# Making every second group of down-projection weight rests on GpSimd in a chain of attention and two gated layers

## The chip, the cores and the metric

One core of a Trainium2 chip runs the whole kernel as one program. The metric is the device time of one execution in microseconds; before the change it is 900.63 us, the median of 3 runs (899.34 to 901.4).

## What is computed

Linear attention with random features, then two feed-forward layers on its output; all data are float32.

```python
# q, k, v: (4, 8, 576, 64); omega: (128, 64)
q_p, k_p = phi(q * scale), phi(k * scale)     # phi: exp of a projection on omega
kv, z = einsum("bhsm,bhsd->bhmd", k_p, v), k_p.sum(2)
x = einsum("bhsm,bhmd->bhsd", q_p, kv) / (einsum("bhsm,bhm->bhs", q_p, z) + 1e-6)
x = x.transpose(0, 2, 1, 3).reshape(2304, 512)
h = x @ w_in                                  # 512 -> 2048
x = (silu(h) @ w_out)                         # 2048 -> 512
g, val = x @ w_gate, x @ w_val                # 512 -> 1536 each
out = (silu(g) * val) @ w_out2                # 1536 -> 512
```

The weights come as 64-bit floats, of which the kernel makes float32.

## The kernel before

The attention takes the first 125 us or so. After it come four stages: an up stage (`up_phase`, x @ w_in), a down stage (`down_phase`, @ w_out), then the same for the second layer with w_gate and w_val, and w_out2. Each matrix product is done by Strassen's scheme in Winograd's form: seven products of half the size in each direction, run in `ORDER` 1, 5, 6, 2, 7, 3, 4. Each operand of a product is split in two parts for TensorE: a lead, which is the operand rounded to a shorter format (`hi`, a copy with ScalarE), and a rest, operand minus lead (`lo`, a subtraction, which writes over the operand). Three matmuls (lead by lead, lead by rest, rest by lead) then stand for one.

A down stage has two kinds of operands.

- The weights of product p, blocks of 128x256. `split_load` (L1244) makes them: SyncE loads a group of up to three blocks (128x768) from `wd_out` in device memory (L1248), ScalarE makes the lead (L1252) and VectorE the rest (L1256). In the first down stage a product has three groups (768, 768 and 512 wide, 21 in all), in the second two of 768 (14 in all). They are made once, stay for all tokens of the stage, and are put into slots of `ra`, `rb` and `rc` as the up stage frees them. Their making begins while the up stage before is at its end. `split_load` also makes the weights of the gate and value products (`w_load`, pieces of 128x448).
- The tokens' operands. `down_phase.split` (L1300 to L1324) treats them in pieces of 128x768 (two feature blocks by 384 tokens); a product has four pieces in the first stage, three in the second, numbered from 0 here. ScalarE makes the lead (L1300) and VectorE the rest (L1304). Where the next product's operand is a difference, VectorE also makes that, piece by piece, after the rest (L1324). SyncE loads the four operands B11, B12, B21, B22 (L1274); the differences T1 to T4 write over them.

A piece is used by 12 matmuls of 128x384 (L1441, six for each of two PSUM banks). Group g of the weights is wanted from the piece on that reaches its three blocks: in the first stage group 0 at piece 0, group 1 at piece 1 and group 2 at piece 3.

On the up stage's side L1091 and L1115 are ScalarE's copies and SiLUs, L1132 and L1148 VectorE's products and sums (most with one input in PSUM), L1100 the stores of its output. GpSimd has the sums of the weight conversion (L376), four a job.

The order on every engine is settled when the program is written. Work waits in streams (`wd` holds the weight loads and splits, `split` the operands, `conv` the conversions); `flush` takes from them, before each group of matmuls, what a model of the engines' clocks says can start soon. The model's costs for an element are in `fixed` (VectorE 0.00106 us, GpSimd 0.0021 us). Each engine then runs its own list in order, and waits for semaphores.

```python
        def lo(o, w):
            h, l = (cut(t, o, w) for t in take())
            nc.vector.tensor_sub(l, l.bitcast(F32), h.bitcast(F32))
```

Of the kernel before, what the change touches and what calls it, by code (L numbers as in the profile page):

```python
# [9 lines left out]
F32 = mybir.dt.float32  # L10
# [32 lines left out]
def kernel(  # L43
# [13 lines left out]
    nc = tc.nc  # L57
# [43 lines left out]
    def cut(t, o, n):  # L101
        return t[:, o : o + n]
# [8 lines left out]
    class Free:  # L111
# [11 lines left out]
        def take(self):  # L123
            assert self.q, f"no {self.name}"
            x, t = self.q.popleft()
            clk["slot"] = max(clk["slot"], t)
            return x
# [12 lines left out]
    def cost(kind, n):  # L140
        a, b = fixed[kind]
        return a + b * n
# [40 lines left out]
    def dma_cost(nbytes):  # L183
        return nbytes / 350e3
# [1036 lines left out]
    def down_ops(m):  # L1221

        fp = FP[m]
        nt = (fp + 2) // 3
        Wd = {}

        def load(p, g):
            o = OPA[PROD[p][0]]
            n = min(3, fp - 3 * g) * 256
            key = lambda *k: ("Wd", m, p, g, *k)  # L1230

            def take():
                if (p, g) not in Wd:
                    Wd[p, g] = (f_op.take(), f_op.take())
                return Wd[p, g]

            return split_load(
                take, n, wd_d[DNK[m]][o, :, g * 768 : g * 768 + n], key, (f_op, 2),
                [(DNK[m], 3 * g + i, "d", (0, 1, 1, 3, 3, 3, 3)[o]) for i in range(n // 256)],
            )  # L1240

        return Wd, [o for p in ORDER for g in range(nt) for o in load(p, g)]

    def split_load(take, n, src, key, slots, ins=(), parts=1):  # L1244


        def load():
            nc.sync.dma_start(out=cut(take()[1], 0, n).bitcast(F32), in_=src)  # L1248

        def hi(o, w):  # L1250
            h, l = (cut(t, o, w) for t in take())
            nc.scalar.activation(h, l.bitcast(F32), AF.Copy)  # L1252

        def lo(o, w):
            h, l = (cut(t, o, w) for t in take())
            nc.vector.tensor_sub(l, l.bitcast(F32), h.bitcast(F32))  # L1256

        ops = [Op("SP", dma_cost(P * n * 4), load, ins=ins, outs=[key("r")], slots=slots)]
        w = n // parts
        for o in range(0, n, w):  # L1260
            end = [key()] if o + w == n else []
            ops += [
                Op("ACT", cost("ACT", w), lambda o=o: hi(o, w), ins=[key("r")], outs=[key("hi", o)]),
                Op("DVE", cost("DVE", w), lambda o=o: lo(o, w), ins=[key("hi", o)], outs=[key("lo", o), *end]),
            ]
        return ops

# [287 lines left out]
    def w_load(k, ins=()):  # L1555
        def take():
            if (k, 0) not in W:
                W[k, 0] = (f_w.take(), f_w.take())
            return W[k, 0]

        return split_load(take, 1792, wu_d[k], lambda *x: ("W", k, 0, *x), (f_w, 2), ins, 4)
# [88 lines left out]
```

## Time and profile before

| | |
|---|---|
| median of 3 runs | 900.63 us (899.34 to 901.4) |
| profiled execution | 901.76 us, its span 900.0 us |
| TensorE busy | 876.9 us, 97% |
| VectorE busy | 628.9 us, 70% |
| ScalarE busy | 548.4 us, 61% |
| GpSimd busy | 161.4 us, 18% |
| TensorE's share of the chain that ended last | 85% |
| VectorE's share of it | 5% |
| first down stage | begins at about 306 us |
| second down stage | begins at about 760 us |

Times in the rows below are microseconds from the start of the span. A row of a timeline gives start, length, engine, line, operation, output and input; neighbours of one kind are merged, and a bracket at the end gives the idle time ahead of the row on its engine and what ended it. An instruction's listed length can begin while the one before it on its engine still runs.

### The profile page before, as it was taken

To read this page: it belongs to the slowest core of one execution; us is meant where nothing else is said; L and a number is where in the kernel's file an instruction comes from. 1 tells how busy PE (TensorE), PEld (TensorE's weight loads), DVE (VectorE), ACT (ScalarE), POOL (GpSimd) and SP (SyncE) were. 2 spreads that over 40 slices of the span, in tenths; PEclk is the share of its full clock that TensorE was granted. 3 is DMA by queue.
4 is the path that set the end of the run, shared out by engine and by line. 5 is a ranking of instruction groups with operands and counts; after the bars stand their busy time and mean duration, and the time that the engine had idled before them with its cause. 6 is when DMAs were issued, how large, how long until landed. Compare 5 with 4: busy or idle time off the path is not lost.

```text
span 900.0 us, 18108 instructions
## 1 busy us (share of the span) xinstructions
PE 876.9 (97%) x6887; PEld 853.0 (95%) x6887; DVE 628.9 (70%) x1016; ACT 548.4 (61%) x1166; POOL 161.4 (18%) x204
## 2 busy tenths in 40 slices
PE   8999999999999989999998999999999999999998
PEld 6787899999999989999998999999999998999998
DVE  3788778576654696785898898555565547968684
ACT  5898878776766764444466856454545356545553
POOL 0474922033441000000000034121212100000000
PEclk9999999999999999999999999999999999999999
DMA  6777448579999937427315557352534278281702
GB/s 200 244 259 240 159 162 271 186 243 303 295 329 343 399 136 220 131 72 237 114 59 181 191 176 243 113 193 99 189 109 154 89 241 285 94 242 44 241 1 71
DMA packets 105863, 170.08 MB, mean 189 GB/s; under 512 B 8752, under 2 KB 87984, under 8 KB 105776
## 3 DMA queue, kind: packets, MB, share of 16 engines
q1 hardware_dynamic: 104608, 168.33, 56.7%
q8 instruction: 54, 0.88, 0.4%
q10 hardware_dynamic: 1168, 0.59, 0.2%
q14 instruction: 33, 0.27, 0.1%
HBM read 107.02 MB, written 61.87 MB: 188 GB/s over the span
## 4 chain that ended last, share of the span: by engine, by line
PE 85%; DVE 5%; ACT 4%; DMA 3%; issue 2%; SPq 0%; DVEq 0%; ACTq 0%
PE ps L1074 45%; PE ps L1441 31%; PE ps L750 3%; PE ps L794 2%; PE ps L810 2%; ACT kq L766 2%; PE ps L841 1%; DMA rawq<-in_q 1%; DVE ra L1304 1%; DMA fa<-in_moe_w_in 1%; DMA fa<-in_moe_w_out 1%; DVE rc L1256 1%; DVE ra L423 1%; DMA ra<-wu_val 1%; DMA om<-in_omega 0%
## 5 line engine op out<-in xcount | busy, mean ns | idle before, releaser
L376 POOL TENSOR_TENSOR fa<-fa 128x256 f32<-128x256 f32 x136 | 111.4, 832 | 554.4 <-DVE fa L357 322.1
L1074 PE MATMUL ps<-ra 128*128 128x384 f32 x840 | 156.2, 335 | 3.5 <-ACT ps L1091 3.5
L1074 PE MATMUL ps<-rb,ra 128*128 128x384 f32 x840 | 157.2, 340 | 0.0
L1074 PE MATMUL ps<-rc,ra 128*128 128x384 f32 x840 | 157.0, 340 | 0.0
L1074 PEld LDWEIGHTS ps<-ra 128*128 128x128 f32 x840 | 146.7, 188 | 4.8 <-ACT ps L1091 4.8
L1074 PEld LDWEIGHTS ps<-rb,ra 128*128 128x128 f32 x840 | 148.8, 188 | 0.3 <-ACT ps L1091 0.3
L1074 PEld LDWEIGHTS ps<-rc,ra 128*128 128x128 f32 x840 | 148.7, 188 | 0.3 <-ACT ps L1091 0.2
L1091 ACT ACTIVATE ps<-ps 128x384 f32<-128x384 f32 x180 | 85.5, 476 | 86.3 <-PE ps L1074 80.1
L1300 ACT ACTIVATE ra<-fa 128x768 fp32r<-128x768 f32 x105 | 87.8, 844 | 81.0 <-PE ps L1441 64.6
L1148 DVE TENSOR_TENSOR fa<-fa,ps 128x384 f32<-128x384 f32 x120 | 66.3, 552 | 100.7 <-ACT ps L1091 73.1
L1304 DVE TENSOR_TENSOR ra<-fa,ra 128x768 fp32r<-128x768 f32 x105 | 100.5, 957 | 48.9 <-PE ps L1441 31.7
L1441 PE MATMUL ps<-ra,rb 128*128 128x384 f32 x720 | 128.5, 339 | 0.0
L1441 PEld LDWEIGHTS ps<-ra,rb 128*128 128x128 f32 x720 | 127.1, 188 | 0.5 <-DVE ra L1304 0.3
L1441 PE MATMUL ps<-ra 128*128 128x384 f32 x612 | 108.8, 335 | 6.7 <-DVE ra L1304 6.5
L1441 PEld LDWEIGHTS ps<-ra 128*128 128x128 f32 x612 | 106.0, 188 | 8.8 <-DVE ra L1304 8.0
L766 ACT ACTIVATE kq<-ps,nb 128x128 f32<-128x128 f32 x288 | 79.1, 408 | 9.8 <-DVE nb L764 8.5
L1441 PE MATMUL ps<-ra,rc 128*128 128x384 f32 x432 | 78.2, 340 | 1.7 <-DVE ra L1304 1.7
L1441 PEld LDWEIGHTS ps<-ra,rc 128*128 128x128 f32 x432 | 76.1, 188 | 2.9 <-DVE ra L1304 2.6
L1115 ACT ACTIVATE fa<-fa 128x384 f32<-128x384 f32 x84 | 43.8, 522 | 28.4 <-DVE fa L1148 28.3
L1324 DVE TENSOR_TENSOR fa<-ra,fa 128x768 f32<-128x768 f32 x63 | 60.1, 954 | 0.7
L1300 ACT ACTIVATE ra<-ra 128x768 fp32r<-128x768 f32 x42 | 35.5, 845 | 34.5 <-PE ps L1441 31.9
L764 DVE TENSOR_REDUCE nb<-ps 128x4 f32<-128x512 f32 x72 | 47.8, 683 | 10.0 <-PE ps L750 5.1
(88 smaller groups left out, 975.6 us busy)
## 6 DMA issues: line engine op xcount, KB each, us to landing
g_d<-fa SPq DMA_DIRECT2D x168, 192.0 KB, 3.6
fa<-g_d SPq DMA_DIRECT2D x42, 384.0 KB, 4.4
ra<-g_d SPq DMA_DIRECT2D x42, 384.0 KB, 4.2
fa<-in_moe_w_out SPq DMA_DIRECT2D x28, 512.0 KB, 5.2
fa<-in_moe_w_in SPq DMA_DIRECT2D x16, 512.0 KB, 5.5
wd_out<-fa SPq DMA_DIRECT2D x14, 512.0 KB, 3.4
fa<-in_moe_w_gate SPq DMA_DIRECT2D x12, 512.0 KB, 3.9
fa<-in_moe_w_val SPq DMA_DIRECT2D x12, 512.0 KB, 5.6
```

The source lines that it names most:

```text
L376: f(blk(f"S{n}"), blk(l), blk(r))
L750: nc.tensor.matmul(ps[2 * (d % 2) + h][t : t + D, o : o + M], raw[u, nm][r, c * P + t : c * P + t + D], om[r, :], start=True, stop=True, s ...
L764: nc.vector.reduce_max(nb, x, axis=AX.X, negate=True)
L766: nc.scalar.activation(e[:, g // 2, g % 2, h * M : (h + 1) * M], x[:, g, :], AF.Exp, bias=nb[:, g : g + 1])
L1074: nc.tensor.matmul(ps[b][:, :N], cut(l, j * P, P), cut(r, j * N, N), start=start and c == 0, stop=stop and c == 5, skip_group_check=True,)
L1091: nc.scalar.activation(out() if callable(out) else out, src, AF.Copy)
L1115: nc.scalar.activation(b["t"], src, AF.Silu)
L1148: nc.vector.tensor_add(t, t if in_place else p5[n], ps[bank_][:, :N])
L1300: nc.scalar.activation(ops[s, p, k][0], src(), AF.Copy)
L1304: nc.vector.tensor_sub(l, src(), h.bitcast(F32))
L1324: (nc.gpsimd if eng == "POOL" else nc.vector).tensor_sub(z(PLACE[to]), z(PLACE.get(l, l)), z(PLACE.get(r, r)))
L1441: nc.tensor.matmul(ps[BANKS[p] + e][:, :N], cut(a, e * P, P), b, start=p in FIRST and i == 0 and c == 0, stop=p in LAST and i == fp - 1 an ...
```

## The change

`split_load` gets a switch that puts the rest on GpSimd and enters GpSimd's cost in the model. `down_ops` sets it for the second group of each product (g = 1); that is seven instructions of 128x768 in each down stage. Group 0, group 2 and the gate and value weights stay on VectorE. Line numbers behind the first added line are one or two higher in the changed kernel: L1252, L1256, L1304 and L1324 become L1253, L1257, L1306 and L1326.

```diff
             return split_load(
                 take, n, wd_d[DNK[m]][o, :, g * 768 : g * 768 + n], key, (f_op, 2),
                 [(DNK[m], 3 * g + i, "d", (0, 1, 1, 3, 3, 3, 3)[o]) for i in range(n // 256)],
+                side=g % 2 == 1,
             )
...
-    def split_load(take, n, src, key, slots, ins=(), parts=1):
+    def split_load(take, n, src, key, slots, ins=(), parts=1, side=False):
...
-            nc.vector.tensor_sub(l, l.bitcast(F32), h.bitcast(F32))
+            (nc.gpsimd if side else nc.vector).tensor_sub(l, l.bitcast(F32), h.bitcast(F32))
...
+        eng = "POOL" if side else "DVE"
...
-                Op("DVE", cost("DVE", w), lambda o=o: lo(o, w), ins=[key("hi", o)], outs=[key("lo", o), *end]),
+                Op(eng, cost(eng, w), lambda o=o: lo(o, w), ins=[key("hi", o)], outs=[key("lo", o), *end]),
```

Since the streams are planned anew, other instructions move too. TensorE's order stays the same. VectorE, where the first down stage begins, before the change (the `rb` rows are, in turn, product 6's third group, product 2's first and second, its third, and product 7's first and second; L1304 is the operand rest of piece 2 of product 1):

```order
L1256 TENSOR_TENSOR rb<-rb 128x512
L1148 TENSOR_TENSOR fa<-fa,ps_83 128x384
L1256 TENSOR_TENSOR rb<-rb 128x768 x2
L1256 TENSOR_TENSOR rb<-rb 128x512
L1256 TENSOR_TENSOR rb<-rb 128x768 x2
L1304 TENSOR_TENSOR ra<-fa,ra 128x768
L1324 TENSOR_TENSOR fa<-fa 128x768
```

and the same place in the changed kernel:

```order
L1257 TENSOR_TENSOR rb<-rb 128x512
L1148 TENSOR_TENSOR fa<-fa,ps_83 128x384
L1257 TENSOR_TENSOR rb<-rb 128x768
L1257 TENSOR_TENSOR rb<-rb 128x512
L1257 TENSOR_TENSOR rb<-rb 128x768
L1306 TENSOR_TENSOR ra<-fa,ra 128x768
L1326 TENSOR_TENSOR fa<-fa 128x768
```

One rest of 128x768 each of products 2 and 7 is gone. ScalarE at the same place, before:

```order
L1252 ACTIVATE rb<-rb 128x512
L1091 ACTIVATE ps_84<-ps_81 128x384
L1252 ACTIVATE rb<-rb 128x768
L1115 ACTIVATE fa<-fa 128x384 x2
L1252 ACTIVATE rb<-rb 128x768
L1115 ACTIVATE fa<-ps_84 128x384
L1252 ACTIVATE rb<-rb 128x512
```

and in the changed kernel:

```order
L1253 ACTIVATE rb<-rb 128x512
L1091 ACTIVATE ps_84<-ps_81 128x384
L1115 ACTIVATE fa<-fa 128x384 x2
L1253 ACTIVATE rb<-rb 128x768
L1115 ACTIVATE fa<-ps_84 128x384
L1253 ACTIVATE rb<-rb 128x768
L1253 ACTIVATE rb<-rb 128x512
```

The lead of product 2's first group moves behind two SiLUs. VectorE where the second down stage begins, before (the first row is product 3's second group, the `rc` rows are product 4's two):

```order
L1256 TENSOR_TENSOR rb<-rb 128x768
L1148 TENSOR_TENSOR fa<-fa,ps_81 128x384
L1256 TENSOR_TENSOR rc<-rc 128x768
L1148 TENSOR_TENSOR fa<-fa,ps_83 128x384
L1132 TENSOR_TENSOR fa<-fa 128x384
L1304 TENSOR_TENSOR ra<-fa,ra 128x768
L1132 TENSOR_TENSOR fa<-fa,ps_84 128x384
L1132 TENSOR_TENSOR fa<-fa 128x384
L1256 TENSOR_TENSOR rc<-rc 128x768
L1324 TENSOR_TENSOR fa<-fa 128x768
```

and in the changed kernel:

```order
L1148 TENSOR_TENSOR fa<-fa,ps_81 128x384
L1132 TENSOR_TENSOR fa<-fa 128x384
L1257 TENSOR_TENSOR rc<-rc 128x768
L1148 TENSOR_TENSOR fa<-fa,ps_83 128x384
L1306 TENSOR_TENSOR ra<-fa,ra 128x768
L1132 TENSOR_TENSOR fa<-fa,ps_84 128x384
L1132 TENSOR_TENSOR fa<-fa 128x384
L1326 TENSOR_TENSOR fa<-fa 128x768
```

Both second groups are gone, and one L1132 stands earlier. GpSimd gets its seven rests of a stage behind the last sums of the conversion that precedes it. ScalarE also takes the leads of the last weights of the first stage (`rc`) earlier among the operand leads, and SyncE issues two of their loads ahead of six operand loads.

## Rows read from the trace of the kernel before

**Rows 1.** Page: busy us with shares, and GpSimd's busy tenths in 40 slices.

```profile
PE 876.9 (97%) x6887; PEld 853.0 (95%) x6887; DVE 628.9 (70%) x1016; ACT 548.4 (61%) x1166; POOL 161.4 (18%) x204
...
POOL 0474922033441000000000034121212100000000
```

**Rows 2.** Timeline of TensorE where the two down stages begin.

```profile
312.38 12.76 PE L1441 MATMUL ps<-ra 128*128 128x384 f32 x72 [0.82 <-DVE ra L1304]
325.99 2.35 PE L1441 MATMUL ps<-ra 128*128 128x384 f32 x12 [0.86 <-DVE ra L1304]
330.67 1.16 PE L1441 MATMUL ps<-ra 128*128 128x384 f32 x5 [2.33 <-DVE ra L1304]
...
761.88 2.36 PE L1441 MATMUL ps<-ra 128*128 128x384 f32 x12 [1.34 <-DVE ra L1304]
765.41 13.62 PE L1441 MATMUL ps<-ra 128*128 128x384 f32 x77 [1.18 <-DVE ra L1304]
```

**Rows 3.** Timeline of VectorE, first down stage.

```profile
307.99 3.46 DVE L1256 TENSOR_TENSOR rb<-rb 128x768 fp32r<-128x768 f32 x4 [0.46 <-ACT rb L1252]
311.37 0.95 DVE L1304 TENSOR_TENSOR ra<-fa,ra 128x768 fp32r<-128x768 f32 x1
312.35 0.96 DVE L1324 TENSOR_TENSOR fa<-fa 128x768 f32<-128x768 f32 x1
...
325.86 3.02 DVE L1256 TENSOR_TENSOR rc<-rc 128x512 fp32r<-128x512 f32 x4
...
329.67 0.95 DVE L1304 TENSOR_TENSOR ra<-fa,ra 128x768 fp32r<-128x768 f32 x1
```

**Rows 4.** Windows: bounds, length, then PE, PEld, DVE, ACT, POOL busy.

```profile
306.50:332.00 25.50, 21.28 (x118) 20.07 (x117) 24.70 (x30) 17.74 (x27) 0.00 (x0) 1.00 0.67 250
```

**Rows 5.** Groups by form, GpSimd: busy us, mean ns of one.

```profile
L423 POOL TENSOR_TENSOR ra<-fa,ra 128x512 fp32r<-128x512 f32 x9 | 11.6, 1296 | 0.0
...
L423 POOL TENSOR_TENSOR ra<-fa,ra 128x256 fp32r<-128x256 f32 x3 | 2.2, 727 | 0.0
```

**Rows 6.** Timelines of VectorE and GpSimd where both run.

```profile
143.34 0.55 DVE L591 TENSOR_TENSOR rb<-fa,rb 128x384 fp32r<-128x384 f32 x1
143.81 1.10 DVE L591 TENSOR_TENSOR rb<-xr,rb 128x384 fp32r<-128x384 f32 x1
...
143.60 0.89 POOL L376 TENSOR_TENSOR fa<-fa 128x256 f32<-128x256 f32 x1 [7.40 <-DMA wd_out<-fa]
...
277.85 0.74 POOL L376 TENSOR_TENSOR fa<-fa 128x256 f32<-128x256 f32 x1
...
277.94 1.47 DVE L1256 TENSOR_TENSOR ra<-ra 128x768 fp32r<-128x768 f32 x1 [0.46 <-ACT ra L1252]
```

**Rows 7.** Timeline of ScalarE, first down stage.

```profile
304.92 0.84 ACT L1252 ACTIVATE rb<-rb 128x768 fp32r<-128x768 f32 x1
...
307.13 0.83 ACT L1252 ACTIVATE rb<-rb 128x768 fp32r<-128x768 f32 x1
...
308.24 2.09 ACT L1252 ACTIVATE rb<-rb 128x512 fp32r<-128x512 f32 x3
310.23 2.30 ACT L1300 ACTIVATE ra<-fa 128x768 fp32r<-128x768 f32 x3
```

**Rows 8.** Timeline of SyncE's DMA issues, first down stage.

```profile
309.57 2.41 SPq L1274 DMA_DIRECT2D ra<-g_d  x3
```

**Rows 9.** Timelines of ScalarE and VectorE, second down stage.

```profile
758.47 0.84 ACT L1252 ACTIVATE rc<-rc 128x768 fp32r<-128x768 f32 x1
...
758.59 0.55 DVE L1148 TENSOR_TENSOR fa<-fa,ps 128x384 f32<-128x384 f32 x1 [0.19 <-ACT ps L1091]
...
760.87 0.95 DVE L1304 TENSOR_TENSOR ra<-fa,ra 128x768 fp32r<-128x768 f32 x1
...
762.67 0.95 DVE L1256 TENSOR_TENSOR rc<-rc 128x768 fp32r<-128x768 f32 x1
...
764.41 0.95 DVE L1304 TENSOR_TENSOR ra<-fa,ra 128x768 fp32r<-128x768 f32 x1
```

## The prediction, made before the changed kernel was run

> **What bounds the kernel now.** The page's busy times come first: TensorE is busy for 97% of the span, and GpSimd's slices are empty from the fourteenth to the twenty-third and in the last eight [rows 1]. Both down stages begin there (at about 306 and 760 us). So only TensorE's gaps can be won. Its timeline shows those that this change can reach, all ended by VectorE's operand rests (L1304): 0.82 us before piece 2 of product 1, 0.86 before piece 0 of product 6, 2.33 before piece 1 of product 6, and in the second stage 1.34 and 1.18 around the first piece of product 1 [rows 2]; 4.0 and 2.5 us in all. From 330.67 and from 765.41 on the timeline has no gap for a long time. A piece is 12 matmuls and takes 2.12 us (six pieces in 12.76).
>
> VectorE's timeline says why [rows 3]. From 307.99 to beyond 330 it does not stop: four weight rests, then operand rest and difference in turn, then weight rests again, four of them at 325.86, and only behind them the operand rest of 329.67 for which TensorE waits longest. Instructions of 128x768 are listed with 0.95 us, but the next begins sooner: from 762.67 two of them take the queue to 764.41, 0.87 each [rows 9]. The window table agrees: VectorE is busy for 24.70 of 25.50 us, GpSimd for none [rows 4].
>
> **What the change takes away.** Fourteen rests of 128x768 leave VectorE, seven in each stage. Whatever stood ahead of 307.99 gives nothing, since VectorE was idle just then for 0.46 us, waiting for ScalarE [rows 3]: products 1, 5 and 6. Four stand in the full stretch: those of products 2 and 7 among the four at 307.99, that of product 3 just ahead of the four at 325.86, that of product 4 among them. They are worth 4 x 0.87 = 3.5 us. In the second stage the rest at 762.67 stands between the two operand rests for which TensorE waits: 0.87 us. The ones ahead of it were followed by a wait for ScalarE (0.19 us at 758.59) and give nothing [rows 9]. If nothing came instead, the sum would be -4.4 us.
>
> **What it adds.** GpSimd has not run this form here. Its nearest rows are 1296 ns for 128x512 and 727 for 128x256, so 2.22 ns a column and 1.87 us for 768 [rows 5]. It is idle, and the first weights that it makes in the full stretch are needed at 330.67 or later, so its own time costs nothing. But it hinders VectorE. At 143.34 VectorE runs two subtractions of 128x384 back to back, all from SBUF, and a GpSimd subtraction begins inside the first. The first takes 0.55, GpSimd ends 0.60 behind it (144.49), and the second, begun at 143.81, ends 0.42 behind GpSimd and is listed with 1.10 [rows 6]. At 277.94 the hindered one is a weight rest itself: GpSimd ends at 278.59, the rest 0.82 later, listed with 1.47 in place of 0.95 [rows 6]. So the two take turns, and a GpSimd instruction of 256 columns holds VectorE for 0.60 us. With 512 columns more at 2.22 ns, one of 768 holds it for 1.7 us. Instructions with an input in PSUM I take as free of this.
>
> The Trainium skill states it as a rule (SBUF — State Buffer, "Who interferes with whom"): a VectorE instruction with two SBUF inputs and a GpSimd instruction that reads SBUF share a read interface, and the one that begins first keeps the other blocked for its whole instruction. By that rule a hold would be the whole 1.87 us and not 1.7, and the four holds below would cost 0.7 us more. The trace agrees on the blocking; its hold of 0.60 us is less than the 0.727 of the whole instruction.
>
> So in the full stretch each moved rest takes away 0.87 us and puts in up to 1.7.
>
> **First stage, step by step.** (a) ScalarE's order changes too: the lead of product 2's first group moves from 304.92 to behind two activations of L1115, to the place at 307.13. From there ScalarE's queue has no gap up to the operand leads that begin at 310.23 [rows 7], so all of it comes 0.8 us later. Product 2's second lead ends at 309.1 and its third at 309.6, product 7's end at 310.4 and 311.2, and piece 2's operand lead at 311.9. (b) GpSimd holds VectorE from 309.2 to 310.95 for product 2. VectorE's rest for product 2's third group waits for that and ends at 311.5. GpSimd's rest for product 7, ready at 311.2, holds for 1.7, product 7's first rest takes 0.82 and the operand rest 0.87: 314.9, whichever of them goes first. Before, it ended at 312.32: +2.5 us. (c) From there to the end of the operand rest for piece 1 of product 6 (330.62) VectorE had 18.3 us of unbroken work. It loses two rests (-1.74) and gets the holds of products 3 and 4, whose leads come before that point (2 x 1.7): +1.7. TensorE needs 7 x 2.12 = 14.8 us for the pieces between and is faster, so VectorE decides at the end of this chain: +4.2. Of each of the four holds I take 0.1 off, since the difference behind an operand rest starts 0.98 after it and not 0.87 [rows 3], a gap that a hold covers: **+3.8 us**.
>
> SyncE's order moves as well: two weight loads go ahead of six operand loads. Three loads were issued in 2.41 us [rows 8], so the six come some 1.6 us later. VectorE comes to the differences that need them 2.5 us later by (b), so this costs nothing. Without holds VectorE would come only 0.6 later (below) and could wait for up to 1 us.
>
> **Second stage.** ScalarE's order stays; product 4's second lead ends at 759.31 [rows 9]. VectorE's L1148 ends at 759.14, and a product of two SBUF tiles (L1132, which now stands next) at 759.6. Then GpSimd holds to 761.3, product 4's first rest ends at 762.15, an L1148 takes 0.47, and the operand rest ends at 763.45 and not at 761.82: +1.6 us. Two times 0.47, a difference and the next operand rest follow, without the rest of 762.67, and end at 766.2 against 765.36: +0.8. If VectorE's rest gets in ahead of GpSimd's, it is +0.4. From there TensorE runs on without a gap. I take **+0.6 us**.
>
> **Sum.** 3.8 + 0.6 = +4.4 us. The profiled execution took 901.76 us (span 900.0, and 1.76 around it), 1.13 above the median of the runs; against that median, 900.63, the forecast is **905.0 us**. Bounds of the unknown cost: with no hold and no late lead -4.4 (896.2); with holds of 1.87, the lead 0.8 late (4 x 1.00 + 0.8) and the second stage at +1.6, +6.4 (907.0).
>
> **Rivals.** *No hold (faster).* GpSimd's rests run beside VectorE's as if alone. VectorE loses 3.5 us of work in the first stage, but the late lead sets its start: the operand rest of piece 2 ends 0.6 late, and 18.3 - 1.74 = 16.5 us of work end at 329.5, 1.1 earlier than before. With 0.8 of the second stage 898.7, and at best 896.2. It decides if a hold costs less than the 0.87 that each move frees. For it speaks that GpSimd stands empty while VectorE is full; against it both places of [rows 6].
>
> *VectorE goes first (no change).* If VectorE's waiting instruction always wins, GpSimd slips until VectorE stops, and only the hold at 309.2 is left, which finds VectorE without work. The operand rest of piece 2 then ends at 313.2, +0.9; the chain behind it is 1.74 shorter; with 0.4 of the second stage 900.2. For it: at 143.81 VectorE's second instruction was begun before the first had ended. Against it: GpSimd got in between all the same [rows 6].
>
> *Holds of whole instructions (slower still).* Up to 907.0, as bounded above.
>
> **How the numbers follow.** A measurement of this kernel can tell about 0.2%, 1.8 us, from no change. The main case, slower, has 0.64, with a range of its own of 902.5 to 907.0; holds of whole instructions have 0.04, no visible change 0.20, the faster case 0.12. So slower 0.68, same 0.20, faster 0.12. The range leaves out most of the faster case and little above: 899.0 to 907.3.
>
> **What would show it.** In the changed profile: GpSimd rests of 128x768 near 1.87 us, longer where VectorE came first; VectorE's subtractions in the full stretch listed with up to 2.5 us in place of 0.95; TensorE's wait before piece 2 of product 1 grown from 0.82 to about 3 us, and those before product 6's first two pieces together still over 3. I am wrong if VectorE's instructions keep 0.95 beside GpSimd's, or if the waits of [rows 2] shrink.

## The result and the profile after

The changed kernel is slower.

| | before | after |
|---|---|---|
| median (9 runs each) | 901.36 us (899.34 to 905.18) | 908.06 us (906.08 to 910.83) |
| ratio, 95% interval | | 1.0076 (1.0059 to 1.0092) |
| profiled execution, its span | 901.76 us, 900.0 us | 909.09 us, 907.3 us |
| mean granted clock of TensorE in it | 1.000 | 0.992 |

The forecast was 905.0 us with a range of 899.0 to 907.3: the sign is right, the time lies above the range. The page of the changed kernel first: busy times, then the granted clock and GpSimd in 40 slices, to be held against [rows 1].

```profile
PE 881.3 (97%) x6887; PEld 857.8 (95%) x6887; DVE 626.8 (69%) x1002; ACT 548.6 (60%) x1166; POOL 188.7 (21%) x218
...
POOL 0474921043333210000000034131212114000000
PEclk9999999999999889999999999999999999999999
```

GpSimd has 14 instructions and 27.3 us more. VectorE has 14 fewer, which at 0.95 [rows 3] are 13 us, but its busy time falls by 2.1 only: what stayed got longer. And the clock row has two slices with an 8, where before there is none. TensorE's timeline where the two down stages begin (as [rows 2]):

```profile
305.47 4.33 PE L1443 MATMUL ps<-ra 128*128 128x384 f32 x24
310.78 0.44 PE L1443 MATMUL ps<-ra 128*128 128x384 f32 x1 [0.98 <-ACT ra L1302]
313.90 13.14 PE L1443 MATMUL ps<-ra 128*128 128x384 f32 x60 [2.69 <-DVE ra L1306]
327.35 2.38 PE L1443 MATMUL ps<-ra 128*128 128x384 f32 x12 [0.31 <-DVE ra L1306]
332.20 4.80 PE L1443 MATMUL ps<-ra 128*128 128x384 f32 x17 [2.47 <-DVE ra L1306]
...
769.06 17.27 PE L1443 MATMUL ps<-ra 128*128 128x384 f32 x89 [3.09 <-DVE ra L1306]
```

The wait before piece 2 of product 1 has grown from 0.82 to 2.69, with 0.98 for ScalarE ahead of it. In the second stage one wait of 3.09 stands in place of 1.34 and 1.18. But the gaps are not all. 60 matmuls, five pieces, take 13.14 us, where before 72 took 12.76 [rows 2]: the instructions themselves became slow. The window table gives the cause in its column behind the five busy times, the granted clock (then DMA share, GB/s):

```profile
311.00:314.00 3.00, 0.32 (x2) 0.10 (x1) 2.97 (x3) 2.56 (x4) 1.16 (x1) 0.74 0.95 359
314.00:317.00 3.00, 3.00 (x10) 3.00 (x11) 3.00 (x4) 0.11 (x1) 0.00 (x0) 0.50 1.06 390
317.00:320.00 3.00, 3.00 (x13) 3.00 (x12) 2.28 (x4) 0.84 (x1) 0.00 (x0) 0.62 1.07 377
320.00:323.00 3.00, 3.00 (x19) 3.00 (x18) 2.70 (x4) 2.12 (x4) 0.00 (x0) 1.00 1.04 398
...
332.00:335.00 3.00, 2.80 (x10) 2.80 (x11) 3.00 (x5) 0.00 (x0) 0.00 (x0) 0.65 0.00 0
...
769.00:772.00 3.00, 2.94 (x11) 2.94 (x12) 2.91 (x6) 0.00 (x0) 0.00 (x0) 0.64 0.98 358
```

In 3 us TensorE does 19 matmuls at clock 1.00 (2.4 GHz) and 10 at 0.50 (1.2 GHz); before has 1.00 over the whole stretch [rows 4]. The trace's clock records have three such stretches in the span beside one at its very end, which before has too: 6.83 us from 312.44, 3.41 from 332.92, 3.41 from 769.83. Each begins inside one of the long waits or up to 0.8 us behind it. Before has none of them.

VectorE at the same places (as [rows 3] and [rows 9]):

```profile
308.56 4.42 DVE L1257 TENSOR_TENSOR rb<-rb 128x512 fp32r<-128x512 f32 x2 [0.67 <-DMA ra<-g_d]
312.90 0.95 DVE L1306 TENSOR_TENSOR ra<-fa,ra 128x768 fp32r<-128x768 f32 x1
...
317.90 0.96 DVE L1306 TENSOR_TENSOR ra<-fa,ra 128x768 fp32r<-128x768 f32 x1 [0.72 <-PE ps L1443]
...
324.90 2.40 DVE L1306 TENSOR_TENSOR ra<-fa,ra 128x768 fp32r<-128x768 f32 x1
327.33 2.48 DVE L1326 TENSOR_TENSOR fa<-ra,fa 128x768 f32<-128x768 f32 x1
...
333.54 0.94 DVE L1306 TENSOR_TENSOR ra<-fa,ra 128x768 fp32r<-128x768 f32 x1
...
760.84 1.60 DVE L1257 TENSOR_TENSOR rb<-rb 128x768 fp32r<-128x768 f32 x1 [0.83 <-ACT rb L1253]
...
764.03 0.56 DVE L1148 TENSOR_TENSOR fa<-fa,ps 128x384 f32<-128x384 f32 x1 [1.05 <-ACT ps L1091]
...
765.09 2.58 DVE L1257 TENSOR_TENSOR rc<-rc 128x768 fp32r<-128x768 f32 x1
...
768.06 0.94 DVE L1306 TENSOR_TENSOR ra<-fa,ra 128x768 fp32r<-128x768 f32 x1
```

and GpSimd, whose rests lie across them:

```profile
308.09 4.08 POOL L1257 TENSOR_TENSOR rb<-rb 128x768 fp32r<-128x768 f32 x2 [4.43 <-ACT rb L1253]
324.23 2.25 POOL L1257 TENSOR_TENSOR rc<-rc 128x768 fp32r<-128x768 f32 x1 [12.07 <-DMA rc<-wd_out]
326.96 2.03 POOL L1257 TENSOR_TENSOR rc<-rc 128x768 fp32r<-128x768 f32 x1 [0.47 <-ACT rc L1253]
...
759.78 1.85 POOL L1257 TENSOR_TENSOR rb<-rb 128x768 fp32r<-128x768 f32 x1 [1.55 <-ACT rb L1253]
762.81 1.85 POOL L1257 TENSOR_TENSOR rb<-rb 128x768 fp32r<-128x768 f32 x1 [1.19 <-ACT rb L1253]
764.82 2.03 POOL L1257 TENSOR_TENSOR rc<-rc 128x768 fp32r<-128x768 f32 x1 [0.15 <-ACT rc L1253]
```

Four VectorE subtractions of 128x768 that meet a GpSimd rest soon after its start are listed with 2.40 to 2.58 in place of 0.95, 1.45 to 1.63 more (one of them is the second of the pair at 308.56). The rest of 760.84 comes 1.06 us after GpSimd's began and is listed with 1.60, 0.65 more. In all five VectorE ends 0.81 or 0.82 us after GpSimd (327.30 after 326.48, 762.44 after 761.63): what VectorE pays is what is left of GpSimd's instruction when its turn comes. The L1148 of 764.03, with one input in PSUM, lies wholly beside the GpSimd rest of 762.81 and neither is longer for it: 0.56 and 1.85.

**A measure that leaves the rest of the kernel out.** TensorE's order is the same in all kernels (but for the unused matmuls of two, which are not counted), so the same matmul can be timed in each. *First stage* below is the time from the first matmul of product 1 to the first that reads the rest of product 6's piece 1 (before: 306.57 to 330.67, 24.10 us; it is the piece's second matmul, the first reads leads alone). *Second stage* is from the up stage's last matmul to the first that reads the rest of product 1's piece 1 (before: 759.76 to 765.41, 5.65). Behind both points TensorE has no gap for a long time in before. Profiles are not compared as wholes, since the time ahead of the first stage differs by up to 4.7 us (303.4 to 308.1 among these kernels; 303.50 and 306.94 in two executions of one, `e4`). The difference from before, for the profiled execution of each kernel in this study (edits and expectations follow):

| kernel | first stage | second stage | median us | ratio to before (95%) |
|---|---|---|---|---|
| the change | +6.08 | +1.59 | 908.06 | 1.0076 (1.0059 to 1.0092) |
| e8, gaps filled | +3.76 | +0.91 | 905.16 | 1.0037 (1.002 to 1.0053) |
| e3, first stage alone | +5.54 | 0.00 | 905.36 | 1.0053 (1.0037 to 1.0069) |
| e4, second alone | +0.04 | +1.96 | 904.77 | 1.0041 (1.0026 to 1.0057) |
| e4 again | +0.05 | +1.95 | 903.11 | 1.0017 (1.0003 to 1.0031) |
| e10, second, gap filled | -0.01 | +0.91 | 901.65 | 1.0004 (0.999 to 1.0019) |
| e5, products 1, 5, 6 | +1.91 | -0.01 | 902.19 | 1.0015 (1.0002 to 1.0028) |
| e2, order alone | +1.54 | +0.93 | 903.16 | 1.0023 (1.0006 to 1.004) |
| e1, rests left out | +1.31 | -0.75 | 899.75 | 0.998 (0.9965 to 0.9995) |
| e6, memset | +2.98 | -0.75 | 899.89 | 0.9992 (0.9975 to 1.0009) |
| e7, one input | +1.90 | +0.13 | 902.05 | 1.0018 (1.0005 to 1.0031) |
| e9, operands first | -3.55 | -0.88 | 901.53 | 1.0003 (0.9987 to 1.0018) |
| e11, operands first, at the starts | -4.56 | -0.87 | 896.31 | 0.9934 (0.9914 to 0.9954) |

Before ran beside them with medians of 900.5 to 901.5.

### The profile page after: what moved, and what is told of

The parts are those of the page before. It is cut to its first block, busy times and chain, and to the rows that moved or that the text cites. A ratio compares the mean times of both kernels' runs of the same rounds, so it can differ in the third digit from the quotient of the medians.

```text
span 907.3 us, 18121 instructions
## 1 busy us (share of the span) xinstructions
PE 881.3 (97%) x6887; PEld 857.8 (95%) x6887; DVE 626.8 (69%) x1002; ACT 548.6 (60%) x1166; POOL 188.7 (21%) x218
## 4 chain that ended last, share of the span: by engine, by line
PE 81%; DVE 7%; ACT 5%; DMA 4%; issue 2%; POOL 1%; SPq 0%; ACTq 0%; DVEq 0%; POOLq 0%
PE ps L1074 41%; PE ps L1443 32%; PE ps L750 3%; ACT kq L766 2%; PE ps L794 2%; PE ps L810 2%; PE ps L841 1%; DVE ra L1306 1%; DMA fa<-in_moe_w_out 1%; DVE fa L357 1%; DVE nb L764 1%; DMA fa<-in_moe_w_in 1%; DVE ra L423 1%; DMA fa<-in_moe_w_gate 1%; POOL fa L376 1%
## 5 line engine op out<-in xcount | busy, mean ns | idle before, releaser
L1074 PE MATMUL ps<-ra 128*128 128x384 f32 x840 | 156.2, 335 | 3.2 <-ACT ps L1091 3.1
L1074 PEld LDWEIGHTS ps<-ra 128*128 128x128 f32 x840 | 146.7, 188 | 4.5 <-ACT ps L1091 4.5
L1306 DVE TENSOR_TENSOR ra<-fa,ra 128x768 fp32r<-128x768 f32 x105 | 102.0, 971 | 52.0 <-PE ps L1443 32.8
L1148 DVE TENSOR_TENSOR fa<-fa,ps 128x384 f32<-128x384 f32 x120 | 66.2, 552 | 103.2 <-ACT ps L1091 79.9
L1443 PE MATMUL ps<-ra 128*128 128x384 f32 x612 | 114.2, 347 | 9.5 <-DVE ra L1306 8.5
L1443 PEld LDWEIGHTS ps<-ra 128*128 128x128 f32 x612 | 111.6, 197 | 11.4 <-DVE ra L1306 9.7
L1326 DVE TENSOR_TENSOR fa<-ra,fa 128x768 f32<-128x768 f32 x63 | 61.6, 978 | 0.7
L1306 DVE TENSOR_TENSOR ra<-ra 128x768 fp32r<-128x768 f32 x42 | 40.2, 958 | 20.9 <-PE ps L1443 9.3
```

What stands on the lines that cost most here:

```text
L1074: nc.tensor.matmul(ps[b][:, :N], cut(l, j * P, P), cut(r, j * N, N), start=start and c == 0, stop=stop and c == 5, skip_group_check=True,)
L1148: nc.vector.tensor_add(t, t if in_place else p5[n], ps[bank_][:, :N])
L1306: nc.vector.tensor_sub(l, src(), h.bitcast(F32))
L1326: (nc.gpsimd if eng == "POOL" else nc.vector).tensor_sub(z(PLACE[to]), z(PLACE.get(l, l)), z(PLACE.get(r, r)))
L1443: nc.tensor.matmul(ps[BANKS[p] + e][:, :N], cut(a, e * P, P), b, start=p in FIRST and i == 0 and c == 0, stop=p in LAST and i == fp - 1 an ...
```

## The experiments

**Does GpSimd hinder VectorE, and by what?** Three kernels keep the order of the changed one and alter only what GpSimd does. In `e1_left_out` nobody makes the 14 rests (these rests are left out of the computation):

```diff
-            (nc.gpsimd if side else nc.vector).tensor_sub(l, l.bitcast(F32), h.bitcast(F32))
+            if not side:
+                nc.vector.tensor_sub(l, l.bitcast(F32), h.bitcast(F32))
```

> The fourteen moved rests are left out altogether (those weights keep their full value where the rest should be); the orders of TensorE, VectorE, ScalarE and SyncE are those of the changed kernel. Theory (GpSimd's instructions hold VectorE, and the TensorE gaps that this makes are followed by half clock): without them 898 to 900.5 us, ratio to before 0.996 to 1.000, no stretch at half clock around 312, 333 or 770 us. Rival (the new order of ScalarE and SyncE costs the time): it stays above 905 us.

899.75 us, a ratio of 0.998. All of VectorE's subtractions in the down stages are back at 0.95. Still the first stage lost 1.31 us, since VectorE, early now, stands still for operand loads, and TensorE behind it; VectorE's and TensorE's rows:

```profile
316.90 0.96 DVE L1327 TENSOR_TENSOR fa<-ra,fa 128x768 f32<-128x768 f32 x1 [1.95 <-DMA ra<-g_d]
```

```profile
318.78 11.41 PE L1444 MATMUL ps<-ra 128*128 128x384 f32 x53 [2.29 <-DVE ra L1307]
```

Behind that 2.29 the clock is 0.5 for 3.41 us, from 320.18; no such stretch was expected. So even free of charge the removal of 14 rests is worth some 0.2% by the ratio, and not the 4.4 us at which the prediction put the rests alone: with them came the new order of ScalarE and SyncE, and the half clock. In the profile the two stages together even lose 0.56 us (+1.31 and -0.75); why the ratio is better than that stays open.

In `e6_memset` GpSimd writes zeros into the 14 rests (which leaves these parts of the products out), and in `e7_one_input` it copies the lead there (which puts the lead in the rest's place), as wide as the rest but reading one operand:

```diff
+            if side:
+                nc.gpsimd.memset(l.bitcast(F32), 0.0)
```

```diff
+            if side:
+                nc.gpsimd.tensor_scalar(l, h.bitcast(F32), 1.0, 1.0, op0=ALU.mult, op1=ALU.mult)
```

> GpSimd writes zeros over the fourteen places (a memset of 128x768, which reads nothing; those weights lose their low part). Theory (GpSimd's reading of SBUF is what holds VectorE): VectorE's subtractions keep 0.95 us and the time is that of the kernel with the rests left out, 898.5 to 901.5 us. Rival (any GpSimd instruction holds VectorE): VectorE's subtractions beside it above 1.3 us.

> GpSimd makes a copy of the lead with one input (128x768) in place of each of the fourteen rests (the weights' low part is wrong then). From 615 ns for 128x512 and 547 for 128x256 such an instruction should take 0.7 to 0.9 us. Theory (VectorE waits as long as GpSimd reads): VectorE's subtractions beside it up to 1.5 to 1.8 us, each hold 0.6 to 0.8, so 899.5 to 903 us. Rival (one input does not hold): all stay at 0.95 us.

GpSimd's and then VectorE's rows of the memset kernel, and of the one-input kernel:

```profile
761.68 0.74 POOL L1258 MEMSET rc<- 128x768 f32 x1 [1.26 <-ACT rc L1253]
```

```profile
761.98 0.95 DVE L1260 TENSOR_TENSOR rc<-rc 128x768 fp32r<-128x768 f32 x1
```

```profile
321.93 0.83 POOL L1258 TENSOR_SCALAR rc<-rc 128x768 fp32r<-128x768 f32 x1 [12.44 <-PE ps L1446]
325.07 1.66 POOL L1258 TENSOR_SCALAR rc<-rc 128x768 fp32r<-128x768 f32 x1 [2.31 <-ACT rc L1253]
```

```profile
321.99 1.58 DVE L1309 TENSOR_TENSOR ra<-fa,ra 128x768 fp32r<-128x768 f32 x1 [0.37 <-PE ps L1446]
325.95 1.59 DVE L1309 TENSOR_TENSOR ra<-fa,ra 128x768 fp32r<-128x768 f32 x1
```

Beside a memset that lies over its first 0.4 us a VectorE subtraction keeps its 0.95, and ends 0.5 after the memset. Beside an instruction that reads one operand it takes 1.58, 0.63 more, while GpSimd needs 0.83 where it comes first; it ends 0.81 after GpSimd (323.57 and 322.76), as beside the true rest. So an instruction of GpSimd that reads holds VectorE to its own end, and the rest, which reads two operands, costs more because it lasts 1.85. The Trainium skill (SBUF — State Buffer, "Who interferes with whom") says that a VectorE instruction with two SBUF inputs meets a GpSimd instruction that reads SBUF, and not one that only writes; these rows agree. The whole times separate the three less well (899.75, 899.89, 902.05), since in all of them VectorE then waits 1.57 to 2.29 us for operand loads in the first stage, and half clock follows. It lasts 6.83 us from 320.75 in the memset's profile and 3.41 in that of `e1_left_out`; that is why the memset's first stage has +2.98 in the table and not +1.31, though no VectorE subtraction is held.

**What does the new order cost by itself?** In `e2_order_on_vector` the planner believes in GpSimd, but VectorE does the work:

```diff
-            (nc.gpsimd if side else nc.vector).tensor_sub(l, l.bitcast(F32), h.bitcast(F32))
+            nc.vector.tensor_sub(l, l.bitcast(F32), h.bitcast(F32))
```

> The order of the changed kernel, but the fourteen rests run on VectorE, at the place at which they were planned for GpSimd. Theory (the hold): VectorE has the same work as before and ScalarE's lead is 0.8 us late, so 901 to 903 us, no VectorE subtraction of 128x768 above 1.1 us in the first down stage, granted clock 1.000 there. Rival (order): above 905 us.

903.16 us, just above the range and well below the rival's, with +1.54 and +0.93 in the stages. VectorE is at 0.95 throughout, the clock is 1.00 in the first stage (in the second it is half for 3.41 us from 766.88, behind a wait of 2.33), ScalarE's operand leads are late as in the changed kernel, and the loads are late here too, by half as much as in `e1_left_out`:

```profile
320.86 0.96 DVE L1326 TENSOR_TENSOR fa<-ra,fa 128x768 f32<-128x768 f32 x1 [0.99 <-DMA ra<-g_d]
```

`e5_slack_only` moves only rests that the prediction called worth nothing, those ahead of a VectorE that waits anyway:

```diff
+                side=g % 2 == 1 and p in ((1, 5, 6), (1, 5, 6, 2))[m],
```

> Only the rests of products 1, 5 and 6 (first stage) and 1, 5, 6 and 2 (second stage) go to GpSimd, those that the prediction called worth nothing, since VectorE waited for ScalarE behind them. Theory (a hold costs time only where VectorE has no slack): 901 +- 1 us, no different from before by more than 0.2%; TensorE's gaps at the start of the down stages as before, the longest 2.3 to 2.4 us. Rival (a GpSimd rest costs wherever it stands, by contention or by the clock of TensorE): 903 us or more.

902.19 us: between the two. No VectorE instruction of the full stretch is held, the second stage is untouched, and the first loses 1.91 us all the same: a planner that thinks VectorE free orders ScalarE and SyncE anew (0.94 us of TensorE's wait there are for a ScalarE lead, and VectorE waits 1.09 for a load), and half clock follows for 3.41 us from 313.54. Where GpSimd's work itself is hidden, the re-ordering still costs, with the clock behind it.

**One stage at a time.** `e3_first_stage` sets the switch by `side=g % 2 == 1 and m == 0`, `e4_second_stage` and `e4_again` by `side=g % 2 == 1 and m == 1`:

> Only the seven rests of the first down stage on GpSimd. Theory (each stage costs by itself): of the +6.8 us about 5 here, so 905 to 907 us, half clock twice between 305 and 340 us. Rival (the two stages meet, for instance through the order of later work): under 904 us.

> Only the seven rests of the second down stage on GpSimd. Theory: +1.2 to +2.2 us, 901.7 to 902.7, one TensorE wait of about 3 us near 766 and half clock behind it. Rival: no change or over 904 us.

> The kernel of the second stage alone once more, beside the next one on the same chip: 904 to 905.5 us, and a profile of another execution. Theory (the granted clock of TensorE makes the difference between the profiled 900.3 us and the median 904.8): a profile of 903 us or more shows more half-clock stretches than the one at 760.47, behind TensorE's gaps there or elsewhere. Rival (the time is lost at full clock): one half-clock stretch or none, and gaps that are longer or more.

The first stage alone costs 5.54 us in the profile and 0.53% in time; the second 1.96 and 1.95 in two profiles. Together that is nearly the whole of the change, 7.50 of 7.67 us. `e3` fell in its range, with half clock twice (313.90 and 330.96). `e4` missed its own: 904.77 us lies above the 901.7 to 902.7 expected, and its repeat, 903.11, below its 904 to 905.5, though the second stage measures the same in both. The profile of the first is its fastest execution (900.3 us), with half clock in a down stage once, at 760.47; that of the second is its slowest (905.86 us), with half-clock stretches at 11.41, 141.11, 332.26 and 765.75. If TensorE loses half of each 3.41 us, three stretches more are an estimated 5.1 of the 5.6 us between the two. The third stands in the first down stage, which is as before in that kernel, behind the wait of 2.31 us that is also there in before ([rows 2], 2.33, with no half clock). The profile of `e4_second_stage` has the same wait (2.33) without half clock. So that wait is sometimes followed by half clock and sometimes not. That all of the spread of 900.3 to 908.8 us comes from this was not shown.

**Is the clock the excess?** `e8_fill` puts unused matmuls into TensorE's waits, on operands long made, into a bank that is free then; 16, 8 and 13 in the first stage, 16 in the second. `e10_second_fill` is `e4` with the 16 alone.

```diff
+        FILL = {(0, 1, 2): 16, (0, 5, 3): 8, (0, 6, 0): 13, (1, 1, 0): 16}
...
+                    fill = FILL.get((m, p, k), 0) if s == 0 else 0
+                    for _ in range(fill):
+                        h = cut(Wd[1, 0][0], 0, N)
+                        nc.tensor.matmul(ps[7][:, :N], cut(h, 0, P), h, start=True, stop=True)
```

> The changed kernel with matmuls of 128x384 added on TensorE into an unused PSUM bank, where its long gaps stood: 16 before piece 2 of product 1, 8 before piece 3 of product 5, 13 before piece 0 of product 6, 16 before piece 0 of product 1 of the second stage (each 0.18 us, so none reaches the end of its gap). Theory (the clock falls after these gaps and costs some 3 us): granted clock 1.000 up to the last microseconds, 904 to 906 us, VectorE still held (subtractions of 2.4 us). Rival (the clock costs nothing, since VectorE sets the pace): 907.5 us or more.

> The second stage alone, with 16 unused matmuls in TensorE's gap ahead of the first piece of product 1. Theory (half clock behind the 3.09 us gap costs 1.7 us and the gap itself 0.6 to 1.7 more): 902 to 903 us, no half clock behind 760. Rival (what the median of 904.8 shows beyond the profile is lost at full clock): 904 us or more, as without the unused matmuls.

905.16 us, less than the change by 2.9 us by the medians and by 3.5 by the ratios, and no half clock but at the very end (900.34). VectorE is held as in the changed kernel:

```profile
306.47 4.46 DVE L1257 TENSOR_TENSOR rb<-rb 128x512 fp32r<-128x512 f32 x2 [0.67 <-ACT rb L1253]
...
322.35 2.49 DVE L1326 TENSOR_TENSOR fa<-ra,fa 128x768 f32<-128x768 f32 x1
...
330.24 0.94 DVE L1306 TENSOR_TENSOR ra<-fa,ra 128x768 fp32r<-128x768 f32 x1
```

TensorE's timeline has the fillers as L1440, and real matmuls at full speed behind them:

```profile
307.54 2.93 PE L1440 MATMUL ps<-ra 128*128 128x384 f32 x16
310.32 0.34 PE L1448 MATMUL ps<-ra 128*128 128x384 f32 x1
311.85 6.58 PE L1448 MATMUL ps<-ra 128*128 128x384 f32 x36 [1.19 <-DVE ra L1306]
318.65 4.26 PE L1448 MATMUL ps<-ra 128*128 128x384 f32 x23 [0.23 <-DVE ra L1306]
```

So the holds and the order cost 3.76 + 0.91 us, and the clock 2.32 + 0.68 on top. In the second stage alone the fillers bring 1.95 down to 0.91 and 903.11 us to 901.65, a little under the 902 to 903 expected; behind 760 the clock is half only at the very end (901.29).

**Can the waits be had otherwise?** The waits come from weight rests that stand ahead of operand rests in VectorE's order. `e9_split_first` is the kernel before with the two streams exchanged in the planner's table, so that ties go to operands:

```diff
     streams = {
         "z": Stream(0.2),
-        "wd": Stream(1.0),
         "split": Stream(1.0),
+        "wd": Stream(1.0),
```

> The kernel before (no rest on GpSimd), with the stream of operand splits put ahead of the stream of weight splits in the planner, so that VectorE's operand rests go ahead of weight rests that are wanted later. Theory (VectorE's order at the stage's start makes TensorE wait 4.0 us there): the waits before piece 2 of product 1 and before product 6 shrink below 1 us in all, 897 to 899 us. Rival (weights then come late and TensorE waits for those): 900 us or more.

901.53 us, above the 897 to 899 expected and where the rival had it. It won 3.55 and 0.88 us in the down stages, and gave it back between them: SyncE's loads moved, and a weight conversion of the second up stage came late, with 6.83 us of half clock around it:

```profile
535.80 1.65 PE L1074 MATMUL ps<-ra 128*128 128x384 f32 x4 [6.17 <-DVE ra L423]
```

`e11_operands_first` exchanges them by a flag where a down stage begins only. All loads stay in the order of before, and VectorE and ScalarE differ only there:

```diff
+                    if swap and name in ("wd", "split"):
+                        i = 3 - i
                     t = max(o.ready(), clk[o.eng]) + 0.1 * i
...
             streams["wd"].extend(wd_ops)
+            swap.append(True)
...
     def hook_d1(s, p, k):
+        if s == 0 and p == 3 and k == 0:
+            swap.clear()
...
             streams["wd"].extend(wd_ops2)
+            swap.append(True)
```

> The kernel before, all rests on VectorE, but where a down stage begins the planner prefers the operands to the weights: by a flag that is set with the weight loads and, in the first stage, taken back at product 3, so that the order of the later conversions and of all loads stays as it is before. VectorE's and ScalarE's orders differ from before at the start of the two down stages alone. Theory (what ends TensorE's gaps is the place of the operand rests in VectorE's order, and not how much of the weights GpSimd takes): the gaps of the first stage fall to one of about 1.4 us and the second stage's by 0.9, as where the preference held everywhere, and no conversion comes late behind it: 4.0 + 2.5 us of gaps less 1.4 and 1.6, so 897 +- 1 us, and no half clock. Rival (the later conversions come late for another reason, the earlier operands themselves): 901 to 902 us with a wait of several us at about 535.

896.31 us: 0.66% less than before, some 1.3% less than the change, and inside the 897 +- 1 of the theory. In its profile no half clock stands in a down stage. TensorE's timeline:

```profile
307.83 10.86 PE L1444 MATMUL ps<-ra 128*128 128x384 f32 x61
318.92 9.48 PE L1444 MATMUL ps<-ra 128*128 128x384 f32 x53 [0.23 <-DVE ra L1307]
...
758.35 2.38 PE L1444 MATMUL ps<-ra 128*128 128x384 f32 x12 [1.34 <-DVE ra L1307]
761.02 2.38 PE L1444 MATMUL ps<-ra 128*128 128x384 f32 x12 [0.29 <-DVE ra L1307]
```

Of 4.0 us of waits in the first stage 0.23 are left where 1.4 were expected, with every rest still on VectorE. VectorE had the time; the order spent it on weights that were not due.

## Why the prediction missed

**The waits and where they are: right.** Both stages lose at the pieces named. Behind the two points of the measure the kernel takes 429.55 and 134.87 us, for 429.09 and 134.57 before.

**(a) ScalarE late: right.** Against the stage's first matmul the lead of piece 2 comes 0.77 us later; 0.8 was forecast.

**(b) Piece 2's operand rest: right.** It ends at 313.85, 8.38 us behind the stage's first matmul, and before at 312.32, 5.75 behind: +2.63 for +2.5.

**The hold: right in kind, a little less in size.** The sum used 1.7 less 0.1 for each of four holds in the first stage; the two at the pair of 308.56 cost 2.7 us together (4.42 for the 1.69 of `e1_left_out`), the other two 1.45 and 1.53. GpSimd alone takes 1.85 for the 1.87 worked out. VectorE is blocked to the end of GpSimd's instruction, as the rival of whole-instruction holds has it, but comes 0.27 to 0.67 us after its start, so the rival's price of 1.87 was not paid and is not the excess. Those of no hold and of VectorE going first are out by the same rows.

**(c) To product 6's piece 1: the failed step.** The prediction counted 2.12 us of TensorE for a piece and concluded that "VectorE decides at the end of this chain". At the waits of 2.69 and 2.47 us the granted clock fell to half, and a piece takes up to twice that. This shows in three places. VectorE, which was to work without a break, waits 0.72 us for TensorE at 317.90. Its rest for piece 1 of product 6 ends at 334.48, +4.96 against the stage's first matmul; the sum had +4.2, and +3.8 with 0.1 off for each hold, so the 0.72 is the larger part of the difference. And TensorE comes to that piece only at 335.64, 1.16 behind the rest: piece 0's 12 matmuls took 3.44 us from 332.20. Hence +6.08 for +3.8. With the waits filled the same stage measures +3.76, and VectorE does decide: in `e8_fill` TensorE comes to the piece 0.06 us behind its rest, which ends at 331.18. That 3.76 and 3.8 agree so closely is in part luck: up to piece 2's rest it is +2.66 and from there +1.1, where the prediction's steps had +2.5 and +1.7 before the 0.4 taken off.

**The second stage: the same step.** The operand rest of piece 0 ends 1.75 late against the stage (forecast +1.6), that of piece 1 at 771.67, 0.88 late (+0.8). But TensorE takes 3.38 us for piece 0 at half clock and begins piece 1 at 772.44: +1.59 for +0.6; filled +0.91, so the clock is 0.68 of it. Of the 0.3 that is left 0.2 is the allowance for VectorE going first, which it did not.

**The loads: mis-sized where it did not count.** That they cost nothing beside holds is right: none of VectorE's differences (L1326) waits for a load in the first stage of the changed kernel up to 334 us. Without holds VectorE waits 0.99 to 2.29 us for them (`e2` the least, `e6` the most), not "up to 1". Whether the faster rival's 898.7, 1.9 us under before, was too low for that is open: with the rests left out altogether the ratio gives 1.8 under, the medians 0.8 under, and the measure of the stages 0.6 over.

**The sum.** 4.4 us were forecast, 4.7 is what both stages lose at full clock, 7.7 with the clock; the medians differ by 6.7, and the ratio says 6.9 (5.3 to 8.3). The range stopped at 907.3 because its upper end took the worst hold and no further mechanism. One piece at half speed in each stage, 2.12 us more each, on top of 905.0 would have put the upper end at 909.2.

## What to carry to other kernels

Moving work to an idle engine frees the full one only by what the two do not contend for: here each subtraction taken off VectorE freed 0.87 us, and in the first down stage its reads on GpSimd put some 1.4 to 1.5 back. Before moving work off an engine that ends the waits, look at what it does first: putting the rests that are due ahead of those that aren't brought 5 us with nothing moved to another engine. And when a change lengthens TensorE's waits, the price is the wait and then the clock behind it.

## What the runs showed of the hardware

- In the down stages of these profiles half clock stands at waits of 1.90 (`e7_one_input`) to 3.09 us, once behind two shorter ones (0.94 and 0.55 us, in `e5_slack_only`), and a wait of 2.3 us in the same place has it in two executions (`e4_again`, `e10_second_fill`) and not in two others (before, `e4_second_stage`). The stretches are listed with 3.41 or 6.83 us.
- Matmuls whose results nobody uses kept the clock at 1.00 through the same waits, and won 2.9 to 3.5 us.
- A GpSimd memset of 128x768 (0.74 us) leaves VectorE alone, a one-input copy (0.83) holds it for 0.63, a subtraction (1.85) for 0.65 to 1.63. A held VectorE subtraction of 128x768 ends 0.81 or 0.82 us after GpSimd's instruction, whenever it came.
